# Weight loads on ScalarE's queue, half of a normalisation on VectorE, and rounding given out earlier: one change to an attention and feed-forward kernel

## Chip, cores and metric

Trainium2, one core of one chip at a time. The metric is the device time of one execution in microseconds (us).

## The reference

```python
# q, k, v: (8, 12, 448, 64) float32; g_q, g_k: (64,)
q_n = q / sqrt(mean(q*q, -1) + 1e-6) * g_q          # k_n likewise with g_k
scores = q_n @ k_n.T / 8
attn = softmax(scores)                              # rows over 448
x = (attn @ v) -> (3584, 768)                       # heads beside each other
h = x @ w_in                                        # (768, 2048)
out = max(h, 0)**2 @ w_out                          # (2048, 768)
```

The weights come as doubles and are rounded to float32 on the chip.

## The kernel before

The kernel works through four spans of two batch entries each. A "pair" is two heads. Both matrix products use a form of Strassen's scheme with seven block products, so rounded weights go through "blocks" (sums and differences of quarters) into a scratch in HBM (`w1s`, `w2s`), from where both products load them again as `sw`.

In span 0 the rounding runs beside the first attention (12 pairs), the first product (56 products) and two pairs "alone" of the next span's attention. It is cut into 35 ticks of four parts each; `weights(n)` runs parts up to number n. What is emitted for an engine stands in its program in that order, and the traces of VectorE, ScalarE and GpSimd show it executed in that order.

```python
EARLY, LATE, ALL = 4 * 12, 4 * 33, 4 * (2 * NFC + 3)

def prepare(t):                                    # one tick; a yield ends a part
    ...
    nc.vector.tensor_scalar(eu, high, 20, 0x7FF, ...)            # L483, part 0
    nc.scalar.activation(f, f, AF.Copy, ...)                     # L486, part 0: what L507 made in the tick before
    total(t - 3, S1, ...); total(t - 3, S2, ...)                 # L478, GpSimd or VectorE
    yield
    nc.scalar.activation(e, eu, AF.Relu, ...); ...               # L493, L494, part 1: need L483
    total(t - 3, S3, ...); total(t - 3, S4, ...)
    yield
    nc.vector.scalar_tensor_tensor(eu, high, ...)                # L501, part 2
    nc.vector.tensor_scalar(high, high, 0xFFFFF, ...)            # L502
    value(t - 2, 0)                                              # L471, GpSimd
    yield
    nc.vector.scalar_tensor_tensor(f, low, 2.0 ** -32, high, ...)  # L507, part 3
    value(t - 2, 1)                                              # L471, GpSimd
    ...                                            # stores of w1s/w2s and loads of raw words, on SyncE
    yield

def norm(i):
    nc.scalar.activation(sq, flat, AF.Square)                    # L584
    nc.vector.tensor_reduce(rflat, sq, ..., ALU.add)             # L587
    nc.vector.tensor_scalar(rflat, rflat, 1.0 / D, 1e-6, ...)    # L588
    nc.gpsimd.tensor_tensor(rflat, rflat, mhalf, ALU.pow)        # L589
    for s in range(2):                                           # q, then k
        nc.gpsimd.tensor_tensor(qkn[:, s], qk[:, s], rstd[:, s], ALU.mult)   # L591

def finish(work, i):
    nc.vector.reciprocal(rec, tots.pop(i))                       # L655
    nc.vector.tensor_tensor(xT[...], pavs.pop(i), rec, ALU.mult) # L656: frees the one pav buffer

def attention(work, first, end, alone):
    for i in range(first, end):
        load(i + 3)                                # q and k, on SyncE
        scores(work, i, 0, alone); scores(work, i, 1, alone)     # PE L621, exponentials on ScalarE L624
        norm(i + 2)
        combine_x(i - 1)
        load_v(i + 1)
        transposes(i + 1, True)                    # PE L607, needs norm(i + 1)
        scores(work, i, 2, alone); scores(work, i, 3, alone)
        take_transposes(i + 1)
        yield                                      # the caller emits rounding here
        values(i, alone)                           # PE L638 (pav) and L649 (tot)
        finish(work, i)
    ...

# callers in span 0
for u, _ in enumerate(attention(work, 0, start_of(1), True)):
    weights(EARLY * (u + 1) // (2 * NPAIR))
for u, _ in enumerate(first_product(work, 0)):
    weights(EARLY + (LATE - EARLY) * (u + 1) // N1)
    ahead(u, start_of(1))
for u, _ in enumerate(attention(work, start_of(1), start_of(1) + ALONE, True)):
    weights(LATE + (ALL - LATE) * (u + 1) // ALONE)
```

## Time and profile before

| | kernel before |
|---|---|
| time, us | 1560.48 median of the first 3 runs (1560.09 to 1562.73) |
| first attention | 156.9 |
| first product of span 0 | 153.4 |
| two pairs alone, up to the first matmul of the second product | 33.9 |
| all that follows | 1215.2 |

The stages are cut on TensorE's timeline: at the first matmul of the first product (`pa`), at the first scores of the pairs alone (`sc`), and at the first matmul of the second product (`ps`). The change touches only the first three. The lines themselves are in the prediction.

### The profile page before, as it was taken

The page shows a single profiled execution, that of the slowest core. Times are in us where ns is not written, and L with a number is a line of the kernel's source. Part 1 is how long each engine was busy: PE and PEld are TensorE (multiplying, and loading weights), DVE is VectorE, ACT ScalarE, POOL GpSimd, SP SyncE. Part 2 cuts the span into 40 slices and gives each one's busy share as a digit, 9 for nine tenths or more (in the row PEclk, how much of TensorE's full clock was granted, in tenths as well). Part 3 has the DMA queues.
Part 4 walks back from the last instruction along what each step waited for, and adds up shares of the span by engine and source line. Part 5 has one row for each costly group of instructions (what it writes and reads, how often), then busy time and mean ns, then how long its engine had stood idle before and what let it go on. Part 6 is the DMA issues. An engine that isn't in the chain of part 4 may idle for free.

```text
span 1559.4 us, 14358 instructions
## 1 busy us (share of the span) xinstructions
PE 1492.1 (96%) x5160; PEld 700.9 (45%) x5160; DVE 764.0 (49%) x874; ACT 481.0 (31%) x670; POOL 514.6 (33%) x367
## 2 busy tenths in 40 slices
PE   6989998879999999999999999999999999999998
PEld 2433444434444455544444445554444444555554
DVE  3778988755655423345555532335555552332011
ACT  4766564533223211223333311223333311111000
POOL 4788577761222002343223102243223301221000
PEclk9999999989999999999999999999999999999999
DMA  5376787742332332333323322332323223323342
GB/s 158 94 222 198 259 288 229 233 153 90 95 89 84 93 94 88 98 99 89 88 82 95 98 82 86 91 99 85 99 80 113 64 64 98 86 86 101 93 110 73
DMA packets 157716, 180.36 MB, mean 116 GB/s; under 512 B 10692, under 2 KB 134084, under 8 KB 157636
## 3 DMA queue, kind: packets, MB, share of 16 engines
q1 hardware_dynamic: 157636, 179.35, 38.2%
q8 instruction: 43, 0.70, 0.2%
q14 instruction: 37, 0.30, 0.1%
HBM read 146.28 MB, written 33.03 MB: 115 GB/s over the span
## 4 chain that ended last, share of the span: by engine, by line
PE 79%; POOL 7%; DVE 5%; DMA 4%; issue 3%; ACT 2%; SPq 1%; POOLq 0%; DVEq 0%; ACTq 0%
PE ps L809 33%; PE sc L621 8%; PE pc L731 8%; PE pd L731 8%; PE pa L731 7%; PE pav L638 4%; DVE acc L629 4%; PE pb L731 4%; PE tot L649 3%; PE pts L607 2%; POOL rstd L589 2%; POOL gC L471 2%; ACT pr L624 2%; DMA sw<-w1s 2%; PE po L797 1%
## 5 line engine op out<-in xcount | busy, mean ns | idle before, releaser
L809 PE MATMUL ps<-gT,sw 128*128 128x448 f32 x768 | 305.7, 545 | 10.4 <-DMA sw<-w2s 10.4
L589 POOL TENSOR_TENSOR rstd<-rstd,mhalf 112x16 f32<-112x16 f32 x48 | 150.0, 3125 | 410.6 <-DVE rstd L588 410.6
L739 POOL TENSOR_TENSOR gT<-gT 128x448 f32<-128x448 f32 x112 | 112.7, 1006 | 465.2 <-ACT gT L735 461.8
L624 ACT ACTIVATE pr<-sc 112x896 f32<-112x896 f32 x192 | 166.2, 915 | 287.0 <-PE sc L621 286.8
L809 PE MATMUL ps<-gC,sw 128*128 128x448 f32 x576 | 230.3, 543 | 0.0
L809 PEld LDWEIGHTS ps<-gT,sw 128*128 128x128 f32 x768 | 142.6, 191 | 146.5 <-issue 134.6
L655 DVE RECIPROCAL rec<-tot 128x448 f32<-128x448 f32 x48 | 142.0, 2958 | 73.4 <-PE tot L649 73.4
L621 PE MATMUL sc<-qkT 64*112 64x448 f32 x768 | 173.4, 571 | 1.9 <-ACT pr L624 1.0
L638 PE MATMUL pav<-pr,vt 112*64 112x448 f32 x768 | 162.5, 546 | 2.7 <-DMA vt<-in_v_dram 2.7
L731 PE MATMUL pa<-xT,sw 128*128 128x448 f32 x384 | 155.7, 542 | 0.5 <-DMA sw<-w1s 0.5
L809 PEld LDWEIGHTS ps<-gC,sw 128*128 128x128 f32 x576 | 105.5, 190 | 101.1 <-issue 99.0
L735 ACT ACTIVATE gT<-gT 128x448 f32<-128x448 f32 x96 | 55.3, 576 | 298.7 <-DVE gT L765 183.3
L629 DVE TENSOR_TENSOR acc<-acc,pr 112x896 f32<-112x896 f32 x68 | 95.8, 1409 | 96.2 <-ACT pr L624 92.3
L591 POOL TENSOR_TENSOR qkn<-qk,rstd 112x512 f32<-112x512 f32 x96 | 117.5, 1245 | 3.8
L731 PEld LDWEIGHTS pa<-xT,sw 128*128 128x128 f32 x384 | 73.0, 191 | 72.3 <-issue 69.2
L621 PEld LDWEIGHTS sc<-qkT 64*112 64x112 f32 x768 | 61.6, 175 | 96.6 <-issue 84.2
L638 PEld LDWEIGHTS pav<-pr,vt 112*64 112x64 f32 x768 | 51.4, 137 | 102.3 <-issue 85.1
L799 ACT COPY osb<-po 112x512 f32<-112x512 f32 x48 | 28.1, 586 | 222.4 <-PE po L797 220.1
L629 DVE TENSOR_TENSOR acc<-pr 112x896 f32<-112x896 f32 x34 | 37.1, 1092 | 119.5 <-ACT pr L624 119.5
L731 PE MATMUL pc<-xC,sw 128*128 128x448 f32 x192 | 81.6, 563 | 5.3 <-DMA sw<-w1s 5.3
L731 PE MATMUL pd<-xT,sw 128*128 128x448 f32 x192 | 80.6, 557 | 4.1 <-DVE z L754 4.1
L731 PE MATMUL pd<-xC,sw 128*128 128x448 f32 x192 | 77.8, 541 | 3.3 <-DVE gT L765 2.1
(84 smaller groups left out, 1486.2 us busy)
## 6 DMA issues: line engine op xcount, KB each, us to landing
sw<-w1s SPq DMA_DIRECT2D x224, 192.0 KB, 2.4
sw<-w2s SPq DMA_DIRECT2D x168, 256.0 KB, 2.8
qk<-in_q_dram SPq DMA_DIRECT2D x48, 224.0 KB, 3.4
qk<-in_k_dram SPq DMA_DIRECT2D x48, 224.0 KB, 3.7
vt<-in_v_dram SPq DMA_DIRECT2D x48, 224.0 KB, 3.4
w1s<-gC SPq DMA_DIRECT2D x8, 1344.0 KB, 6.0
w2s<-gC SPq DMA_DIRECT2D x24, 448.0 KB, 3.7
out_dram<-osb SPq DMA_DIRECT2D x48, 224.0 KB, 2.9
```

What stands on the lines that cost most here:

```text
L589: nc.gpsimd.tensor_tensor(rflat, rflat, mhalf, ALU.pow)
L591: nc.gpsimd.tensor_tensor(qkn[:, s].rearrange("p j h d -> p h j d"), qk[:, s].rearrange("p h (j d) -> p h j d", d=D), rstd[:, s].rearrange ...
L621: nc.tensor.matmul(sc[:, h, 0:S], qkT[rows, 1, c * SP:(c + 1) * SP], qkT[rows, 0, :], start=True, stop=True)
L624: nc.scalar.activation(pr, sc[:, :, 0:S], AF.Exp)
L629: nc.vector.tensor_tensor(accs[i], probs[i, 0] if c == 1 else accs[i], pr, ALU.add)
L638: nc.tensor.matmul(pavs[i][h * D:(h + 1) * D, :], vs[i][:, h, c, :], pr[:, h, :], start=(c == 0), stop=(c == NJ - 1))
L649: nc.tensor.matmul(tots[i][h * D:(h + 1) * D, :], ones, pr[:, h, :], start=first, stop=last)
L655: nc.vector.reciprocal(rec, tots.pop(i))
L731: nc.tensor.matmul(ps, stream[n][:, c], rhs[:, c], start=first and c == 0, stop=c == HC - 1, skip_group_check=not first)
L735: nc.scalar.activation(g, src, AF.Relu)
L739: nc.gpsimd.tensor_tensor(g, g, g, ALU.mult)
L809: nc.tensor.matmul(ps, stream[n][:, c % 4], rhs_of[i][:, c], start=c == 0, stop=c == HF - 1)
```

## The change

Its intent is threefold. Loads of rounded blocks in the first product shall no longer stand behind stores in SyncE's queue. GpSimd, late in the first attention, gives the k half of the normalisation to VectorE and takes more rounding. The last ticks are given out before the second pair alone. The `alone` switch is also on in the two pairs alone of span 1, so the k half goes to VectorE there too.

```diff
-    EARLY, LATE, ALL = 4 * 12, 4 * 33, 4 * (2 * NFC + 3)
+    EARLY, LATE, ALL = 4 * 14, 4 * 33, 4 * (2 * NFC + 3)
...
-            nc.sync.dma_start(sw.rearrange("p c m -> p (c m)"), src)
+            queue = nc.scalar if len(stream) < N1 else nc.sync
+            queue.dma_start(sw.rearrange("p c m -> p (c m)"), src)
...
-    def norm(i):
+    def norm(i, alone=False):
...
-            nc.gpsimd.tensor_tensor(
+            (nc.vector if alone and s else nc.gpsimd).tensor_tensor(
...
-                norm(i + 2)
+                norm(i + 2, alone)
...
-    norm(0)
+    norm(0, True)
...
-        norm(1)
+        norm(1, True)
...
-                weights(LATE + (ALL - LATE) * (u + 1) // ALONE)
+                weights(ALL)
```

## The prediction

> **What bounds the kernel now.** The span is 1559.4 us with TensorE (PE) busy 1492.1, so all idle time of PE together is 67 us. I cut the span where the first product's first weight block, the attention after it, and the second product begin on PE, and took busy time per stretch:
>
> ```profile
> 0.00:156.87 156.87, 133.56 (x673) 54.26 (x673) 105.46 (x109) 96.57 (x120) 112.31 (x79) 0.99 0.57 169
> 156.87:310.27 153.40, 138.40 (x344) 66.66 (x344) 128.44 (x149) 84.68 (x118) 107.49 (x82) 0.94 0.76 254
> 310.27:344.18 33.91, 22.82 (x121) 9.06 (x121) 22.46 (x23) 15.93 (x21) 26.28 (x18) 0.92 0.53 167
> 344.18:1559.40 1215.22, 1197.31 (x4024) 570.96 (x4024) 507.61 (x596) 283.81 (x411) 268.49 (x189) 1.00 0.31 90
> ```
>
> The columns are the stretch and its length, then busy PE, weight loads, VectorE (DVE), ScalarE (ACT), GpSimd (POOL), then granted clock, DMA share, GB/s. Stretch one is the first attention, two the first product of span 0, three the two pairs "alone". The change touches only these. PE idles 23.3 + 15.0 + 11.1 = 49.4 us there, and the clock dips in two and three; the last 1215 us stay.
>
> Next I asked for PE's groups by line in each stretch, for their idle time and what ended it (here the lines with most of it; the first from stretch one, the last from three):
>
> ```profile
> L607 PE MATMUL pt<-ident,qkn 112*128 112x112 f32 x96 | 14.6, 292 | 19.0 <-POOL qkn L591 19.0
> ...
> L638 PE MATMUL pav<-pr,vt 112*64 112x448 f32 x192 | 45.3, 548 | 2.7 <-DMA vt<-in_v_dram 2.7
> ...
> L731 PE MATMUL pc<-xC,sw 128*128 128x448 f32 x48 | 23.5, 635 | 5.3 <-DMA sw<-w1s 5.3
> L731 PE MATMUL pd<-xT,sw 128*128 128x448 f32 x48 | 22.5, 611 | 4.1 <-DVE z L754 4.1
> ...
> L809 PE MATMUL ps<-gT,sw 128*128 128x448 f32 x1 | 1.1, 1116 | 10.4 <-DMA sw<-w2s 10.4
> ```
>
> The 19.0 us on POOL hold 12.6 us of start; 6.4 are later stalls. In the first product, DMA of weight blocks costs 8.8 us in all groups, DVE about 6.3. The means 635 and 611 ns against 539 ns undisturbed add some 8 us: after the longer stalls the matmuls run slow. At the end one wait of 10.4 us stands for the last rounded w_out block.
>
> Last I read VectorE's and GpSimd's timelines for one pair of the first attention:
>
> ```profile
> 73.06 2.96 DVE L655 RECIPROCAL rec<-tot 128x448 f32<-128x448 f32 x1 [2.46 <-PE tot L649]
> 76.05 0.62 DVE L656 TENSOR_TENSOR xT<-pav,rec 128x448 f32<-128x448 f32 x1
> 76.70 1.22 DVE L587 TENSOR_REDUCE rstd<-qkn 112x16 f32<-112x1024 f32 x1
> 77.95 0.91 DVE L588 TENSOR_SCALAR rstd<-rstd 112x16 f32<-112x16 f32 x1
> ...
> 83.52 2.96 DVE L655 RECIPROCAL rec<-tot 128x448 f32<-128x448 f32 x1 [1.03 <-PE tot L649]
> ```
> ```profile
> 67.75 4.01 POOL L589 TENSOR_TENSOR rstd<-rstd,mhalf 112x16 f32<-112x16 f32 x1 [2.23 <-DVE rstd L588]
> 71.84 2.04 POOL L591 TENSOR_TENSOR qkn<-qk,rstd 112x512 f32<-112x512 f32 x2
> 73.84 4.01 POOL L478 TENSOR_TENSOR gC<-gC 128x384 f32<-128x384 f32 x4
> 77.79 3.28 POOL L471 TENSOR_TENSOR gC<-gT,gC 128x384 f32<-128x384 f32 x2
> ```
>
> A pair takes 10.46 us (73.06 to 83.52). VectorE idles only 1.0 to 2.5 of it. GpSimd is oversubscribed: 13.3 us in this stretch, its wait of 2.2 us before. GpSimd's lateness holds the w1s store in SyncE's queue, the q and k loads behind it, and so every second late pair (13.1, 13.0, 15.6 us where others take 10.5).
>
> **What the skill says.** (1) "Perfetto Trace Analysis", Tensor Engine Instruction: ACT, DVE and GpSimd are strict FIFO. The trace agrees: the reciprocal starts after everything emitted before it. (2) "SBUF — State Buffer", Who interferes with whom: a VectorE op in a 2-port mode, or with two SBUF inputs against GpSimd's reads, shares one port pair with GpSimd and the later one waits. The trace fits: this L588 took 0.91 us with GpSimd busy, 0.17 elsewhere, and the pow 4.01 us beside rounding, 2.9 alone. (3) "DMA: Bandwidth & Descriptors", Issuing engines are not separate DMA queues: a second issuing engine saves only issue time on the same 16 engines. The change's gain must therefore come from SyncE's in-order waits. They are there: its waits for GpSimd's and VectorE's rounding before w1s and w2s stores sum to 106 us from 76 to 345 us, and weight-block loads stand behind them. (4) "TensorE: Matmul & The Clock Gate", What's actually happening: idle windows of about 3.4 us halve the clock. The trace has slow matmuls already after 1.94 and 3.4 us of idle (4.19 and 4.82 us for six, normally 2.42).
>
> **The change part by part.**
>
> *k on VectorE.* GpSimd loses one qkn of 1.02 us per pair. VectorE gains one of 112x512; from its own 112x448 (0.61 us) and 112x896 (1.09) I interpolate 0.68. But its place is what matters: VectorE must now stand from L588 until GpSimd's pow (2.9 us) is done, in order, before rounding and before the next reciprocal; and the reciprocal and xT free the one buffer that PE's next values need. VectorE's ring per pair: 2.96 + 0.62 + 1.22 + 0.17, pow 2.9 with two hand-overs 0.15, k 0.68 and perhaps 0.3 behind GpSimd's q half, rounding 3.05 (0.55 + 0.96 + 0.57 + 0.96, undisturbed) x 14/12 = 3.6, gaps 0.2. Sum **12.8 us** against 10.46. I walked it through: first reciprocal at 30.5 (0.7 sooner, since the start's k half now runs beside q), second at 43.3, the tenth eight rings later, plus 3 x 0.62 for xC: 147.5. The last two pairs have no norm: 10 us each, end near 168. PE's stalls behind POOL and late q/k/v go (GpSimd has 9 us of work in 12.8), but the stage ends near 168 instead of 156.9. Allowing for overlap I missed, **+10 us**.
>
> *14 ticks and the queue.* The first product now holds 19 ticks instead of 21 in its 56 products. VectorE's 128.4 us busy, of which 8 x 5 x 0.61 = 24 is its own adds, becomes about 24 + 104 x 19/21 = 118. PE needs 56 x 6 matmuls at 0.376 = 127 us undisturbed, and took 153.4. With sw loads on ScalarE's queue, each waits only for the product four back and for no store: the 8.8 us of DMA idle go, and about 5 us of slow matmuls with them. Of VectorE's 6.3 us and 4 us of slow clock I keep nearly all: the largest (3.0 us) comes from a norm of the next span, unchanged. ScalarE pays 56 issues of about 0.4 us (22 us, 85 us busy of 153 before: it fits, but delays squares and exponent steps by perhaps 2 us in all), and the first five blocks are issued only after its last attention work, not 7 us ahead: +1. Sum -8.8 - 5 - 1 (lighter VectorE) + 2 + 1 = **-12 us** (rounded).
>
> *The rest sooner.* Before, GpSimd rounds the last block at 332.6 to 334.6, after the norm of the second alone pair (pow at 326.9, qkn to 332.6). Now both ticks precede that norm: pow 317.7, q to 321.6, two values to 323.7, totals to 326.3. The stores go 8 us sooner. But VectorE's reciprocal of the first alone pair stands behind them, at about 324.8 instead of 321.7, so PE's next values start 2.7 us later, and the sw loads stand in SyncE's queue behind q/k loads that wait for the second norm (ready about 334). First second-product matmul near 338 instead of 344.2: -6, and about 1.5 of the 2.5 us that its first 16 matmuls lost to the clock: **-7.5 us**.
>
> Sum: +10 - 12 - 7.5 = -9.5; from 1560.5, **about 1552 us** in round numbers.
>
> **Rivals.** *A: the pow wait is hidden.* If VectorE reaches L588 early enough, the attention stays at 157 or falls to 148 (the 6.4 + 2.7 us of stalls gone). For it: GpSimd was the late engine. Against: VectorE idles only 1.0 to 2.5 us per pair, and the wait is over 3. Time 1533 to 1542. *B: ScalarE becomes the bound of the first product.* Its issues wait for PE and hold back exponents that VectorE needs, so the DMA idle only changes its name. For it: the skill's shared engines and a 3.0 us stall that already follows a late square; against: ScalarE is 55% busy there. The -12 shrinks to -3; time 1561. *C: VectorE's ring is longer,* 13.5 us or more with port conflicts: attention +17, time 1559.
>
> **Range and chances.** The terms are uncertain by about 5, 5 and 2.5 us, together some 8. Range 1537 to 1564. Faster by 2% needs under 1529.9, more than all three gains with no loss in the attention: 0.04. Slower by 2% (over 1592) needs both losses far larger: 0.02. Within 2%: 0.94.
>
> **What would show it.** Right: VectorE idle of about 3 us before the k half, released by GpSimd's pow; reciprocals 12.5 to 13.3 us apart; first product starting 8 to 13 us later; no sw<-w1s idle over 1 us inside the first product, which lasts 138 to 145 us; the w2s wait below 4 us. Wrong: pairs still 10.5 us apart (rival A), or ScalarE waits ending PE's idle in the first product (B).

## More of the kernel before

Lengths of stages come from the one profiled execution of each kernel, which in some cases was 2 to 4 us faster than the median; differences between stages are good to about that. The experiments ran on two chips, with the kernel before in every round; it took 1561.6 to 1561.9 us on both.

## The result and the profile after

1571.59 us median of 4 runs (1570.81 to 1574.09), against 1561.61 (1560.09 to 1564.22) of the kernel before on the same chip: ratio 1.0065, 95% interval 1.0046 to 1.0084. Slower by 10 us, and outside the forecast range.

The busy times of the changed kernel in the same four stretches (columns as in the prediction):

```profile
0.00:185.71 185.71, 141.53 (x672) 55.20 (x673) 128.66 (x129) 102.57 (x126) 120.37 (x75) 0.94 0.52 158
185.71:327.77 142.06, 132.15 (x344) 65.03 (x344) 120.61 (x140) 80.12 (x113) 97.14 (x76) 0.96 0.76 254
327.77:357.10 29.33, 24.58 (x121) 9.48 (x120) 17.09 (x17) 15.31 (x21) 18.89 (x13) 0.94 0.61 185
357.10:1569.70 1212.60, 1195.00 (x4024) 569.99 (x4024) 512.23 (x603) 284.08 (x412) 273.88 (x192) 1.00 0.31 90
```

The first attention grew by 28.8 us (156.9 to 185.7), the first product shrank by 11.3 (153.4 to 142.1), the pairs alone by 4.6, the remainder by 2.6 (its first 16 matmuls take 6.28 us instead of 8.58). The sum is the 10.3 us by which the profiled span grew. So all of the loss lies in one stage.

PE's groups with idle time, in the first attention (the first three) and the first product:

```profile
L623 PE MATMUL sc<-qkT 64*112 64x448 f32 x192 | 50.9, 656 | 20.4 <-ACT pr L626 19.1 <-ACT qkT L615 1.4
L640 PE MATMUL pav<-pr,vt 112*64 112x448 f32 x192 | 47.9, 580 | 7.6 <-DVE xT L658 7.6
...
L609 PE MATMUL pt<-ident,qkn 112*128 112x112 f32 x96 | 13.3, 288 | 15.3 <-POOL qkn L593 15.3
...
L733 PE MATMUL pa<-xT,sw 128*128 128x448 f32 x96 | 39.5, 548 | 2.3 <-DMA sw<-w1s 2.3
L733 PE MATMUL pd<-xT,sw 128*128 128x448 f32 x48 | 21.9, 596 | 7.2 <-DVE z L756 7.2
```

The waits for GpSimd's `qkn` and for late v loads did shrink, almost to the start alone. In their place PE waits 19.1 us for the exponentials on ScalarE and 7.6 for VectorE's `xT`. In the first product the DMA idle fell from 8.8 to 2.5 us, and one wait of 7.2 us for VectorE took part of its place: its sum `z` stood behind a wait of VectorE of 6.2 us for raw words of w_out. (Line numbers are 2 higher than before from L584 on.)

One full ring of VectorE, from reciprocal to reciprocal, in the changed kernel:

```profile
58.55 2.94 DVE L657 RECIPROCAL rec<-tot 128x448 f32<-128x448 f32 x1
61.52 0.62 DVE L658 TENSOR_TENSOR xT<-pav,rec 128x448 f32<-128x448 f32 x1
63.15 1.22 DVE L589 TENSOR_REDUCE rstd<-qkn 112x16 f32<-112x1024 f32 x1 [1.00 <-ACT qkn L586]
64.40 0.17 DVE L590 TENSOR_SCALAR rstd<-rstd 112x16 f32<-112x16 f32 x1
67.59 0.69 DVE L593 TENSOR_TENSOR qkn<-qk,rstd 112x512 f32<-112x512 f32 x1 [3.01 <-POOL rstd L591]
68.20 0.95 DVE L501 SCALAR_TENSOR_TENSOR gC<-gT,gC 128x768 uint32<-128x768 uint32 x1
69.19 1.28 DVE L502 TENSOR_SCALAR gT<-gT 128x768 uint32<-128x768 uint32 x1
70.50 1.66 DVE L507 SCALAR_TENSOR_TENSOR gT<-gT 128x768 f32<-128x768 uint32 x1
72.08 1.37 DVE L483 TENSOR_SCALAR gC<-words 128x768 uint32<-128x768 uint32 x1
73.38 2.94 DVE L657 RECIPROCAL rec<-tot 128x448 f32<-128x448 f32 x1
```

The ring is 14.83 us long and VectorE waits for PE nowhere in it: the reciprocal, which before waited 0.6 to 2.5 us for `tot` in the same pairs, now follows the rounding at once. The two stops are 3.01 us for GpSimd's pow and 1.00 us for ScalarE's square. What GpSimd does beside VectorE's k half and rounding, its q half and two values:

```profile
67.63 2.42 POOL L593 TENSOR_TENSOR qkn<-qk,rstd 112x512 f32<-112x512 f32 x1
70.02 3.02 POOL L471 TENSOR_TENSOR gC<-gT,gC 128x384 f32<-128x384 f32 x2
```

Before, in the early pairs, VectorE rounded beside the pow instead: the first pow in the prediction's lines ran from 67.75 to 71.76, VectorE's rounding from 67.58 to 70.60. ScalarE in the changed kernel's stretch:

```profile
72.19 0.92 ACT L486 ACTIVATE gT<-gT 128x768 f32<-128x768 f32 x1 [5.43 <-DVE gT L507]
73.49 0.94 ACT L493 ACTIVATE gC<-gC,clamp 128x768 f32<-128x768 uint32 x1 [0.38 <-DVE gC L483]
74.46 0.93 ACT L494 ACTIVATE gC<-gC,clamp 128x768 uint32<-128x768 f32 x1
75.30 1.71 ACT L626 ACTIVATE pr<-sc 112x896 f32<-112x896 f32 x2
```

ScalarE stands 5.43 us for VectorE's L507, and the exponentials at 75.30, whose scores PE had finished at 73.3, come after it. This is a second loop: VectorE late, then ScalarE's rounding, then exponentials and the next square, then VectorE's reduction.

### The profile page after: what moved, and what is told of

It reads as the page before. It is cut to its first block, busy times and chain, and to the rows that moved or that the text cites. A ratio compares the mean times of both kernels' runs of the same rounds, so it can differ in the third digit from the quotient of the medians.

```text
span 1569.7 us, 14351 instructions
## 1 busy us (share of the span) xinstructions
PE 1493.3 (95%) x5160; PEld 699.7 (45%) x5160; DVE 778.6 (50%) x886; ACT 482.1 (31%) x670; POOL 510.3 (33%) x355
## 4 chain that ended last, share of the span: by engine, by line
PE 75%; DVE 8%; POOL 8%; issue 5%; DMA 2%; ACT 2%; SPq 0%; ACTq 0%; POOLq 0%; DVEq 0%
PE ps L811 32%; PE pd L733 8%; PE pa L733 8%; PE pc L733 8%; PE sc L623 6%; DVE acc L631 4%; PE pb L733 4%; PE pav L640 3%; POOL rstd L591 2%; POOL gC L471 2%; PE tot L651 2%; PE pts L609 2%; POOL qkn L593 2%; POOL gC L478 1%; PE po L799 1%
## 5 line engine op out<-in xcount | busy, mean ns | idle before, releaser
L591 POOL TENSOR_TENSOR rstd<-rstd,mhalf 112x16 f32<-112x16 f32 x48 | 142.4, 2968 | 418.3 <-DVE rstd L590 418.2
L623 PE MATMUL sc<-qkT 64*112 64x448 f32 x768 | 177.8, 583 | 20.5 <-ACT pr L626 19.1
L640 PE MATMUL pav<-pr,vt 112*64 112x448 f32 x768 | 166.1, 557 | 10.5 <-DVE xT L658 10.5
L657 DVE RECIPROCAL rec<-tot 128x448 f32<-128x448 f32 x48 | 141.8, 2955 | 47.4 <-PE tot L651 47.4
L733 PE MATMUL pa<-xT,sw 128*128 128x448 f32 x384 | 155.6, 541 | 2.3 <-DMA sw<-w1s 2.3
L593 POOL TENSOR_TENSOR qkn<-qk,rstd 112x512 f32<-112x512 f32 x82 | 122.5, 1511 | 3.8
L631 DVE TENSOR_TENSOR acc<-pr 112x896 f32<-112x896 f32 x34 | 37.1, 1091 | 119.5 <-ACT pr L626 119.5
L615 ACT ACTIVATE qkT<-pts,gains 128x448 f32<-128x448 f32 x68 | 39.4, 631 | 132.8 <-PE pts L609 132.8
```

Source lines behind the costliest of these rows:

```text
L593: (nc.vector if alone and s else nc.gpsimd).tensor_tensor(qkn[:, s].rearrange("p j h d -> p h j d"), qk[:, s].rearrange("p h (j d) -> p h ...
L615: nc.scalar.activation(qkTs[i][:, s], pt, AF.Copy, scale=gains[:, s:s + 1])
L623: nc.tensor.matmul(sc[:, h, 0:S], qkT[rows, 1, c * SP:(c + 1) * SP], qkT[rows, 0, :], start=True, stop=True)
L631: nc.vector.tensor_tensor(accs[i], probs[i, 0] if c == 1 else accs[i], pr, ALU.add)
L640: nc.tensor.matmul(pavs[i][h * D:(h + 1) * D, :], vs[i][:, h, c, :], pr[:, h, :], start=(c == 0), stop=(c == NJ - 1))
L733: nc.tensor.matmul(ps, stream[n][:, c], rhs[:, c], start=first and c == 0, stop=c == HC - 1, skip_group_check=not first)
```

## The experiments

Theory R: the loss is VectorE's ring, which the stand behind the pow made the bound. Rival T: the 14 ticks, which are not a whole number per pair (4 or 5 parts), made it. After the first results, S and V split up what the ticks add: S the cut through a tick, V the plain volume. Fourteen kernels ran. Stage lengths of all of them, in us, from the profiled executions:

| kernel | median | first attention | first product | pairs alone | remainder |
|---|---|---|---|---|---|
| before | 1561.6 to 1561.9 | 156.9 | 153.4 | 33.9 | 1215.2 |
| after | 1571.59 | 185.7 | 142.1 | 29.3 | 1212.6 |
| k_only | 1575.09 | 170.0 | 155.6 | 31.7 | 1215.4 |
| no_k | 1549.18 | 161.3 | 141.5 | 29.6 | 1213.4 |
| ticks_only | 1556.50 | 160.9 | 144.8 | 33.2 | 1215.7 |
| queue_only | 1565.91 | 158.1 | 159.0 | 32.5 | 1215.2 |
| whole_ticks | 1570.38 | 181.7 | 140.6 | 29.7 | 1212.7 |
| k_late | 1549.48 | 160.5 | 140.8 | 29.3 | 1214.4 |
| no_k_whole | 1556.03 | 169.2 | 142.2 | 29.5 | 1213.6 |
| ticks_sooner | 1550.05 | 161.7 | 144.3 | 28.9 | 1213.1 |
| sooner_only | 1556.70 | 157.9 | 153.2 | 30.0 | 1213.6 |
| no_k_13 | 1554.20 | 160.2 | 149.8 | 29.4 | 1213.0 |
| no_k_16 | 1549.53 | 170.6 | 135.4 | 28.5 | 1213.6 |
| no_k_late35 | 1555.55 | 162.2 | 151.7 | 24.9 | 1214.4 |
| no_k_tail | 1553.73 | 167.5 | 141.8 | 30.0 | 1213.0 |

(k_quiet is told below.)

### One part alone: k_only, ticks_only, queue_only, sooner_only

k_only is the kernel before with the `norm` edits of the change and nothing else.

> Before plus only the k half on VectorE. Theory R (the wait for pow stands in VectorE's ring): every norm pair of the first attention takes 13.2 to 13.9 us instead of 10.5, the first product starts 15 to 22 us later than in the kernel before, nothing is gained later, time 1575 to 1583. Theory T (the 14 ticks, which split a round of rounding between two pairs, made the attention long, and the k half is harmless): pairs stay at 10.5 us, the late-load stalls go, time 1553 to 1561.

Measured: ratio 1.0089 (1.0072 to 1.0106), attention 170.0 us. R, though the ring (12.9 us) and the growth of the stage (13.1) are a little smaller than it said. VectorE's timeline of k_only, one ring:

```profile
70.08 2.94 DVE L655 RECIPROCAL rec<-tot 128x448 f32<-128x448 f32 x1
...
78.03 0.69 DVE L591 TENSOR_TENSOR qkn<-qk,rstd 112x512 f32<-112x512 f32 x1 [3.01 <-POOL rstd L589]
...
80.10 1.30 DVE L502 TENSOR_SCALAR words<-words 128x768 uint32<-128x768 uint32 x1
81.43 1.65 DVE L507 SCALAR_TENSOR_TENSOR words<-words 128x768 f32<-128x768 uint32 x1
82.99 2.94 DVE L655 RECIPROCAL rec<-tot 128x448 f32<-128x448 f32 x1
```

82.99 - 70.08 = 12.91 us, and so in every full pair before the xC subtractions begin. PE waits 17.7 us for `xT`. With whole ticks PE waits 0.3 us for exponentials.

ticks_only changes one number:

```diff
-    EARLY, LATE, ALL = 4 * 12, ...
+    EARLY, LATE, ALL = 4 * 14, ...
```

> Before plus only 14 ticks in the first attention. R: VectorE and GpSimd get 2 more ticks (about 0.6 and 0.8 us a pair), partly in slack, and the first product gets 2 fewer; attention +3 to +8, first product -2 to -6, time 1558 to 1565. T: attention +15 us or more, time 1570 or more.

Measured: ratio 0.9975 (0.9958 to 0.9993). The attention pays 4.0 us, the first product gives back 8.6, more than either theory said, so the time lies 1.5 us below R's range. T falls: the ticks alone do not lengthen the attention by 15 us.

queue_only has the two `queue` lines of the change alone.

> Before plus only ScalarE's queue for the first product's weight blocks. If the loads stood behind the store waits of SyncE's queue: the attention unchanged (157 us), DMA idle inside the first product from 8.8 to under 3 us, that stage 153 to 141-146 us, time 1549 to 1554. If the engines' transfers were the limit, the waits stay and the time is 1558 to 1563.

Measured: ratio 1.0020 (1.0003 to 1.0036): slightly slower, which neither side expected. The loads do land sooner (median 3.3 us from issue against 5.4) and PE's DMA idle in the first product falls from 8.8 to 4.9 us. But VectorE's longest wait in that stage (total us, times, longest) shows what follows:

```profile
DVE gC L483 <- DMA words<-in_moe_w_out_dram: 5.8, 1, 5.8
```

Before, VectorE's waits for raw words of w_out came to 3.2 us in three pieces (1.5, 1.1 and 0.6, by the buffer they went to). Now it waits 5.8 us at once, with the sum `z` behind it, and PE then stands 6.0 us. In all, PE's idle behind `z` grows from 4.1 to 13.8 us. The raw words of w_out land a little later (6.6 us against 6.2 median, 7.5 against 6.3 for those in `gC`), but this one wait is no slow landing: SyncE issued the words from 295.69 on, after waiting 4.3 us for GpSimd's values (L471), which read these buffers, and VectorE went on at 301.10, at most 5.4 us after the issue. Here the order of work delayed them; why it shifted, and what delayed the others, is not settled.

sooner_only has `weights(ALL)` alone.

> Before plus only the sooner rest. In the kernel with 14 ticks it took the end from 33.2 to 28.9 us and the second product's slow start 2.6 us less. If it works alone as well: attention 157 and first product 153 us unchanged, end 28 to 30 us, time 1553 to 1557. If the two pairs alone are held up instead (their second values wait 3.5 us for VectorE): 1559 or more.

Measured: ratio 0.9972 (0.9956 to 0.9989). It works alone: end 30.0 us, and the second values wait 3.5 us for VectorE as forecast.

### One part undone: no_k, and the queue: ticks_sooner

no_k is the changed kernel with `nc.gpsimd.tensor_tensor(` in place of the choice between engines.

> The changed kernel with the k half back on GpSimd; 14 ticks, ScalarE's queue and the sooner rest stay. R: the attention comes back to 155 to 164 us, the gains of the first product (about -11) and of the end (about -5 to -7) stay, time 1543 to 1552. T: the attention stays near 180 us, time 1566 to 1572.

Measured: ratio 0.9921 (0.9905 to 0.9938). R: without the k half, the same change is some 12 us faster than the kernel before instead of 10 slower. The attention is 161.3 us, so 24.4 of its 28.8 us depend on the k half.

ticks_sooner is ticks_only with `weights(ALL)`; it differs from no_k only by the queue.

> Before plus 14 ticks and the sooner rest, with neither the k half nor ScalarE's queue: differs from the run without the k half only by the queue. If the queue pays once the first product's rounding is lighter: first product near 144.8 us against 141.5, time 1551 to 1555 against 1549.2. If the queue is worth nothing even then (alone it cost 4 us): time 1545 to 1549.

Measured: ratio 0.9928 (0.9911 to 0.9944). The first product is 144.3 against 141.5 us, but the medians differ by 0.9 us, inside the runs' scatter. The queue is worth at most 3 us even with 14 ticks. The reason is the same as in queue_only: without the queue PE stands 10.0 us for weight blocks in that stage and never for `z`, with it 1.7 us for blocks and 7.3 for `z`.

### The stand behind the pow: k_late

The k half stays on VectorE, but is emitted behind the pair's rounding (`scale(s, engine)` is the multiplication by `rstd`, s = 1 for k; lines condensed):

```diff
+    put_off = []
     def norm(i, alone=False):
...
+        scale(0, nc.gpsimd)
+        if not alone: scale(1, nc.gpsimd)
+        elif i < 2:   scale(1, nc.vector)
+        else:         put_off.append(lambda: scale(1, nc.vector))
...
                 yield
+                while put_off:
+                    put_off.pop()()
             values(i, alone)
```

> The changed kernel, with the k half still on VectorE but emitted behind the pair's rounding and ahead of its reciprocal, so that the pow runs while VectorE rounds. If the stand behind the pow is what the k half costs: VectorE's 37.1 us behind the pow fall below 8, the ring is 10.6 to 11.5 us, attention 157 to 166, time 1543 to 1553. If the cost is VectorE's extra 0.69 us and conflicts with GpSimd: attention 175 or more, time 1561 or more.

Measured: ratio 0.9925 (0.9909 to 0.9942), attention 160.5 us. VectorE of k_late:

```profile
80.74 0.96 DVE L507 SCALAR_TENSOR_TENSOR words<-words 128x768 f32<-128x768 uint32 x1
82.90 0.69 DVE L595 TENSOR_TENSOR qkn<-qk,rstd 112x512 f32<-112x512 f32 x1 [1.20 <-POOL rstd L593]
83.51 2.95 DVE L666 RECIPROCAL rec<-tot 128x448 f32<-128x448 f32 x1
```

This ring is 10.55 us (the reciprocal before stands at 72.96); the later ones are 10.6 to 16.3 us, as no_k's are 10.5 to 17.0. The waits for the pow fell from 37.1 to 17.4 us, 6 of them at the start, not below 8 as expected; one of 3.8 us remains where GpSimd is late. So 25 us of attention hang on where one operation of 0.69 us stands in VectorE's order, not on its work. The place does two things at once: VectorE no longer stands, and it rounds beside the pow again instead of beside the q half and the values (L502 takes 0.56 us in this ring, 1.28 in the changed kernel's; L507 0.96 against 1.66). k_late does not tell the two apart; k_quiet below sizes the second. But k_late is no faster than no_k: hidden, the move brings nothing.

### Parts or whole ticks: whole_ticks, no_k_whole, no_k_tail

whole_ticks and no_k_whole give out whole ticks, two of them in the sixth and twelfth pair:

```diff
-                weights(EARLY * (u + 1) // (2 * NPAIR))
+                weights(EARLY // 4 * (u + 1) // (2 * NPAIR) * 4)
```

> The changed kernel, but its 14 ticks are given out whole: one tick a pair, two in the sixth and twelfth pair, never 4 or 5 parts. With the k half alone (12 whole ticks) the ring of VectorE was 12.92 us and the attention 170.0 us; with 14 ticks in parts 185.7. Theory S (the split of ticks makes ScalarE wait for VectorE inside a pair, with the exponentials and the next square behind it): rings back at 12.9 us but for one long pair, PE's 19.1 us behind the exponentials below 6, attention 173 to 178, time 1559 to 1564. Theory V (the volume of two more ticks in a ring that is already full): attention 181 to 187, time 1567 to 1573.

Measured: median 1570.38, 1566.4 to 1572.5; ratio 1.0061 (1.0043 to 1.0079), not to be told from the changed kernel. PE in the attention:

```profile
L640 PE MATMUL pav<-pr,vt 112*64 112x448 f32 x192 | 47.5, 575 | 20.8 <-DVE xT L658 20.8
...
L623 PE MATMUL sc<-qkT 64*112 64x448 f32 x192 | 46.5, 606 | 6.5 <-ACT pr L626 4.9 <-ACT qkT L615 1.5
```

S is right about the mechanism: waits for exponentials fall from 19.1 to 4.9 us and the rings with one tick return to 12.9 to 13.5 us. But the wait changes its name to `xT` (20.8 us), and the sixth pair's ring is 18.9 us. On time, V wins: VectorE's ring is full, and the two ticks cost much the same in both arrangements. The cut may cost up to 4 us by the stage lengths; the medians do not show it.

> The changed kernel without the k half on VectorE and with whole ticks. S: PE's waits behind the exponentials (5.1 us in the run without the k half) go, but two pairs hold two ticks; attention 156 to 162 against 161.3, time 1544 to 1550. V: attention stays at 161 to 163, time 1548 to 1551.

Measured: ratio 0.9961 (0.9944 to 0.9977), attention 169.2 us, a miss for both. Without the k half, parts are better than whole ticks by 7 us: 4 or 5 parts a pair fit better into VectorE's slack than a lump of 8, with which the sixth pair's ring is 20.5 us long.

no_k_tail puts the two extra ticks into the last two pairs, which have no norm:

```diff
-                weights(EARLY * (u + 1) // (2 * NPAIR))
+                weights(4 * (u + 1 + max(0, u - 9)))
```

> The changed kernel without the k half on VectorE, and its two extra ticks put into the last two pairs, which have no norm; all other pairs hold one whole tick. If an extra tick is cheap where VectorE has slack: attention 157 to 161 against 161.3 spread evenly, first product 141 to 144, time 1544 to 1549. If the two last pairs are stretched by a whole tick each: attention 164 to 167, time 1551 to 1555.

Measured: ratio 0.9949 (0.9931 to 0.9966), attention 167.5 us. The last intervals between reciprocals are 19.3 and 15.2 us. The slack is not there either. And 4.8 us of the 167.5 are PE's wait for the first weight block (0.7 in no_k): ScalarE issues the first five blocks only behind its last rounding of the stage, at 163.96.

### Conflicts inside the ring: k_quiet

k_only with GpSimd's rounding left out in the first attention. The result is wrong (relative error 1.2).

```diff
+            if t < EARLY // 4:
+                return                       # in value(): nothing on GpSimd
...
-            if there(n) and n % 2:
+            if there(n) and n % 2 and late:  # in total()
...
+        nc.gpsimd.memset(stage[:, 0:BLOCKS * 8 * HW], 0.0)
```

> Only the k half on VectorE (12 whole ticks), and GpSimd's share of the rounding left out in the first attention; the result is wrong on purpose (half of the first product's weights are zeros or scraps), and a clearing of the blocks delays the start by some us, so only the distance of VectorE's reciprocals counts. If conflicts with GpSimd's rounding lengthen VectorE's rounding in the ring: the four operations return from about 0.55, 0.96, 1.28 and 1.66 us to 0.55, 0.96, 0.57 and 0.96, and the ring from 12.92 to 11.4 to 11.7 us. If the lengths belong to VectorE's own operands: still 12.9.

VectorE of k_quiet (its L504 and L509 are L502 and L507 of k_only):

```profile
71.08 2.95 DVE L657 RECIPROCAL rec<-tot 128x448 f32<-128x448 f32 x1
...
81.10 1.29 DVE L504 TENSOR_SCALAR words<-words 128x768 uint32<-128x768 uint32 x1
82.43 0.96 DVE L509 SCALAR_TENSOR_TENSOR words<-words 128x768 f32<-128x768 uint32 x1
83.31 2.95 DVE L657 RECIPROCAL rec<-tot 128x448 f32<-128x448 f32 x1
...
152.87 0.56 DVE L504 TENSOR_SCALAR words<-words 128x768 uint32<-128x768 uint32 x1
```

The ring is 12.23 us instead of 12.91: the fourth operation returned to 0.96 us, the third stayed at 1.29. Half of what was expected. GpSimd's rounding thus costs the ring 0.7 us a tick. The other 0.7 us stay where only the q half of the norm is left on GpSimd, which is itself drawn out to 2.9 us there. The last two pairs of the same run have no norm, so no q half, and GpSimd does nothing beside them: there the third operation takes 0.56 (the last line) and 0.57 us. So the other 0.7 us are the q half's.

### The best exchange: no_k_13, no_k_16, no_k_late35

no_k with `EARLY` at 4 * 13 and 4 * 16, and with `LATE` at 4 * 35.

> The changed kernel without the k half on VectorE and with 13 ticks. 14 ticks cost the attention 4.4 us and gave the first product 11.9 with the queue, 12 ticks with the queue lost 5.6 there. If the exchange is even per tick: attention 158 to 160, first product 144 to 150, time 1551 to 1556; if 13 is the best: below 1548.

> The same with 16 ticks. If the attention's slack is used up at 14 (about 1.7 us a pair on VectorE, of which two ticks take 0.8): attention 167 to 173, first product 132 to 138, time 1547 to 1554. If slack is left: attention below 165, time below 1546.

> The same with 14 ticks and all of the rest already given out in the first product (35 ticks by its end, none in the pairs alone). If the 3.5 us by which the second pair alone waits for VectorE come from the rest standing there: the wait goes, end 24 to 27 us, first product 144 to 149, time 1546 to 1551. If VectorE only falls behind in the first product: that stage 150 or more, time 1553 or more.

Measured: ratios 0.9956, 0.9921 and 0.9959. 13 ticks are 5 us slower than 14. From 14 to 16 ticks the attention loses 9.4 us (161.3 to 170.6) and the first product wins 6.1, yet the medians are equal (1549.5 and 1549.2), so the exchange is even there to within the profiles' error. With all of the rest in the first product, the 3.5 us wait of the second values goes and the end is 24.9 us, but the first product takes 151.7, so it costs more than it saves. no_k, k_late, no_k_16 and ticks_sooner lie within 0.9 us of each other, 0.7 to 0.8% ahead of the kernel before; none of the fourteen is better.

## Why the prediction was wrong

**The place of the loss: right.** "VectorE must now stand from L588 until GpSimd's pow (2.9 us) is done, in order". It does, for 3.0 us in each pair (once 3.85), and k_late shows that the place behind the pow is what costs.

**The size of the loss: wrong, and this is the step that failed.** "Sum 12.8 us against 10.46 ... +10 us". Measured +28.8. The ring of 12.8 us was forecast for 14 ticks, but 12.91 us is what k_only has with 12. The term that failed is the rounding, "3.05 (0.55 + 0.96 + 0.57 + 0.96, undisturbed) x 14/12 = 3.6". In the eight pairs from 53 to 163 us the rounding, from the end of the k half to the reciprocal, took 5.18, 5.18, 7.46, 5.24, 4.36, 5.62, 5.19 and 5.19 us (xC subtractions left out), 5.4 on average. Over these pairs that is 14.6 us more than forecast, most of the 17.7 by which the stage ended after the 168 of the prediction's walk. The durations came from pairs in which VectorE rounded beside GpSimd's pow, and there it was the pow that was drawn out (4.01 us against 2.9), not VectorE's operations. The k half behind the pow moves the rounding to where the q half and the values run: both engines are released by the same pow, in every pair. There L502 and L507 take 1.28 and 1.66 us instead of 0.57 and 0.96, and k_quiet puts 0.7 us a tick on GpSimd's rounding and 0.7 on the q half. The prediction named this conflict and quoted 0.91 against 0.17 us for it, but put only 0.3 us for it into the sum (on the k half) and left the rest to rival C.

Second, the ring was held to contain VectorE and GpSimd only. ScalarE is in it: its L486 and L493 wait for VectorE's rounding, and exponentials and the next square stand behind them. Where a pair's parts cut through a tick, VectorE waits 1.0 us for that square (three such pairs), and PE 19.1 us for exponentials. whole_ticks took these waits away, but hardly any time, because the volume of 14 ticks kept the ring full.

A rough account of the stage: the k half +13.1 us (k_only 170.0), two more ticks in a ring already full +11.7 (whole_ticks 181.7), the cut +4.0 (185.7). The middle step also brings in the queue, with 2.1 us of wait for the first weight block that k_only does not have; and the profiled execution of whole_ticks was 4.0 us faster than its median, so less may belong to the cut. The same two ticks cost 4.0 to 4.4 us where VectorE still had slack (ticks_only, no_k). The prediction's ring had the k half and the ticks in one sum, but at undisturbed lengths: two ticks more were 0.5 us of ring there, some 6 us over twelve pairs.

**The start: wrong by a little.** "0.7 sooner, since the start's k half now runs beside q": the first reciprocal came 0.8 us later (31.97 against 31.21). The q half on GpSimd took 1.55 us beside the k half instead of 1.02, but the delay has another cause: the square of pair 1 waited for its k load until 14.09 instead of 13.35. Kernels whose start is as before (no_k, ticks_only, no_k_whole, no_k_tail) have it anywhere from 30.47 to 32.59, so this term can't be read from single executions.

**The first product: right size, wrong cause.** Forecast -12, measured -11.3. Nearly all of it was ascribed to the queue, "-8.8 - 5", and 1 us to lighter rounding. ticks_only gives -8.6 without the queue, queue_only +5.6 without the ticks. Rival B was nearer for the queue: the DMA idle changed its name, though mainly through late raw words on VectorE, not through a busy ScalarE. The -12 was thus met by luck.

**The end: right.** -7.5 forecast, -4.6 and -2.6 measured. Stores came sooner, the second values waited 3.0 us (forecast 2.7), and the w2s wait fell to 1.8 us (forecast below 4).

**The rivals.** A was refuted by every kernel with the k half at its place. C, "13.5 us or more with port conflicts: attention +17, time 1559", was the nearest but still short: the eight full rings took 14.7 us on average (xC subtractions in three), with ScalarE in them. The chance of 0.94 for "within 2%" holds; the direction does not. Three slips in the prediction's numbers change nothing: the third late pair took 15.9 us (130.75 to 146.64), not 15.6; 56 x 6 matmuls at 0.376 us are 126.3, not 127; and its times (1552, 1561, 1559) fit a start of 1561.1, the mean of the first three runs, not the median 1560.5 that it names.

## What to carry to other kernels

Before an engine is given an operation, see whom that operation waits for and what stands behind it in the same engine's order. Here 0.69 us of work cost 13 us over a stage, by waiting and by moving the work behind it beside another engine's, and nothing measurable when it stood behind the pair's rounding. When a change moves work in time, take its durations from a place where the neighbours do what they will then be doing. And run each part alone: three of the four parts together were worth -12 us, hidden under one part worth +22 (no_k against the changed kernel).

## What the Trainium skill lacked or had wrong

- "SBUF — State Buffer", Who interferes with whom, says that the later of two contenders blocks until the first has finished. The q half on GpSimd (1.02 us alone) took 2.9 us in k_only's pairs, longer than any one VectorE operation beside it (0.69, 0.55 and 0.95 us in a row): its length fits a wait through several operations in a row, which the page does not tell.
- "DMA: Bandwidth & Descriptors", Issuing engines are not separate DMA queues, says that a second issuing engine saves only issue time. Issuing the 192 KB blocks from ScalarE, which the profile of queue_only lists under a queue of its own (q10 beside q1), cut their median time from issue to landing from 5.4 to 3.3 us, while raw words in `gC` went from 6.3 to 7.5. So more than issue time changed.
- "TensorE: Matmul & The Clock Gate", What's actually happening, gives a window of about 3.4 us of idle. In queue_only, six matmuls took 4.13 us after 2.20 us of idle (granted clock 0.60 over them), and 2.52 us after 2.30 (clock 1.00). So idle well below the window can slow them, and not each time. Whether the window's free running explains that, no run here shows; the page's advice in Why this matters for your kernels is only against gaps over some 3 us.
- No page has the duration of a GpSimd pow: 2.9 us for 112x16 elements with VectorE standing, up to 4.6 us in the kernel before with VectorE rounding beside it.
